# Gate and value of the last 1024 tokens as seven products of half matrices, in a fused attention and two-MLP kernel

## The chip, the cores and the metric

The kernel runs on one core of a Trainium2 chip. The metric is the device time of one execution in microseconds (us). Five engines work side by side, each through its own queue in order: PE (TensorE, matrix multiply), DVE (VectorE), ACT (ScalarE), POOL (GpSimd) and SP (SyncE, which here only issues DMAs). Work on different engines is ordered by semaphores alone.

## The reference

```python
x = attention(q, k, v)            # 4 batches, 8 heads, 576 positions, 64 per head, block mask of 64
x = x.transpose(0, 2, 1, 3).reshape(2304, 512)
g = x @ w_gate                    # 512 x 1536
x = (g * (1 / (1 + exp(-g))) * (x @ w_val)) @ w_out      # 1536 x 512
h = x @ w_in                      # 512 x 2048
out = where(h > 0, h, exp(min(h, 0)) - 1) @ w_out2       # 2048 x 512
```

All of it is in float32 terms. Weights come as 64-bit words and are turned into float32 on the chip. Each float32 matmul of the MLPs is made of three matmuls of rounded halves: high by high, high by low, low by high (`mm3`, L181 to L184).

## The kernel before

The 2304 tokens are cut into nine chunks of 256. The program is one Python list of tasks. `Plan.order` (L85) gives each task an engine, a duration and a priority, schedules the list in its own model of time and writes the instructions in the order that it finds. Nothing is reordered afterwards: an instruction that waits holds up all that stand behind it on its engine.

- **Attention** (`a_pair`, `a_head`, L392 to L540) works on 32 pairs of heads, four per chunk, and alternates between a short form (320 keys) and a long form (576 keys). A pair has scores on PE (L430), then mask, maximum and its scaling on DVE (L478, L483, L486), two exponentials per head on ACT (L495), reciprocals of the sums on DVE (L499, L501), the scaling of the probabilities by them on DVE (`norm`, L503; the line of ACT in it is taken for heads below `NACT`, which is 0), transposes on PE (L530, L531, L441), copies of them on ACT (L535, L445) and the product with the values on PE (L452). The scores of one pair stand in two PSUM tiles, `sa` and `sb`, with no second buffer. ACT and DVE then split the result into `xh` and `xl` (L461, L464).
- **Gate and value** (`gv_pair`, L545): for each chunk and each of 12 blocks f of 128 features, 24 matmuls of 256 columns into one PSUM tile `gv` (two buffers). ACT takes a tanh of the gate half (L563), DVE two steps (L567, L572), and pairs of blocks go out to DRAM (`a_scr`).
- **First output product** ("p2", `p2_unit`, L609): `a_scr` comes back, is split (L592 on ACT, L595 on DVE), and 512-column matmuls accumulate into `y`.
- **Second MLP** ("p3", `p3_h` and `p3_o`): the input product is already done by seven products of half matrices (`M1` to `M7`). Sums of weight halves are formed by `p3_weights` (L712: sums on DVE, high half on ACT, low half on POOL) and go to DRAM and back.

Gate and value matmuls have later priorities than the attention of the chunks that follow, so they fill PE wherever attention waits. With nine chunks of them, the last attention pair is spread until 324 matmuls, a little over one chunk, of them are left.

Of the kernel before, what the change touches and what calls it, by code (L numbers as in the profile page):

```python
# [8 lines left out]
F32 = mybir.dt.float32  # L9
# [14 lines left out]
CH = 256  # L24
NCH = NT // CH
QW = 256
# [8 lines left out]
UNIT0, UNIT, LEAD1, LEAD2, LEAD, CLEAD, CSTEP = 3.2, 3.4, 25.0, 40.0, 40.0, 20.0, 0.8  # L35
GF, NACT, NTH = 4, 0, 8
# [91 lines left out]
def attention_moe_moe_kernel(ctx: ExitStack, tc: tile.TileContext,  # L128
# [6 lines left out]
    y_scr = [dram.tile([KD, 128, 2 * HT], F32, name=f"y_scr{c}") for c in range(NG)]  # L135
    w_scr = [dram.tile([7, 128, 512], F32, name=f"w_scr{p}") for p in range(HP)]
# [36 lines left out]

    def cv_hi(i):
        act.copy(cv_units[i][1], cv_state[i][1])

    def cv_lo(i):
        _, hi, lo = cv_units[i]
        pool.tensor_tensor(lo, cv_state.pop(i)[1], hi.bitcast(F32), ALU.subtract)  # L179
# [40 lines left out]
    def tr_t():  # L220
# [4 lines left out]
    plan = Plan(dict(raw=3, rawb=2, c=4, rk=2, rq=2, rv=3, nm=4, sm=4, pl0=4, pl1=4, ph=4, th=NTH, tt=2, x=3, sa=1, sb=1, tp=2, gv=2,  # L225
                     th1=2, s2=2, st=2, ar=5, ah=3, y=6, ys=4, ws=NW, wm=3, gp=NP, et=2, hc=4))
# [3 lines left out]
    pl_t = {g: [attn.tile([128, e], F32, name=f"pl{g}{i}") for i in range(4)] for g, e in ((0, 256), (1, 512))}  # L230
    ph_t = [attn.tile([128, S], F32, name=f"ph{i}") for i in range(4)]
# [3 lines left out]
    ph1.tile([128, 80], F32, name="padw")  # L235
    t0 = sb("t0", 1)
    lo_r, hi_r = slice(0, 64), slice(64, 128)
    xh_c, xl_c = {}, {}

    def x_alloc(c):  # L240
        if c not in xh_c:
            xh_c[c] = x_p.tile([128, KD, CH], F32R, tag="xh", name="xh", bufs=3)
            xl_c[c] = x_p.tile([128, KD, CH], F32R, tag="xl", name="xl", bufs=3)


    def conv_unit(i, prio, after=(), whole=False):
        r, c, w = ("raw" if i < 2 * K1 else "rawb", i, 0), ("c", i, 0), ("w", i, 0)
        add("SP", 450, lambda: cv_dma(i), prio, writes=[r] + ([("raw", i, 0)] if 2 * K1 <= i < 2 * K1 + 2 else []), data=1900 if i == 1 else 1430)
# [9 lines left out]
    qz = [t0.tile([128, H, 128], F32, name=f"qz{u}") for u in range(2)]  # L258
    kz = [t0.tile([128, H, D], F32, name=f"kz{u}") for u in range(2)]
    vz = t0.tile([128, 16, 128], F32, name="vz")  # L260
    qd = [t0.tile([128, H, D], F32, name=f"qd{u}") for u in range(2)]
# [16 lines left out]
    def t0_init():  # L278
# [4 lines left out]
        for i in range(4):  # L283
            add("POOL", 190, lambda i=i: pool.memset(pl_t[0][i][:, 192:256], 0.0), PT0, writes=[("plz", 0, i)])
            add("POOL", 190, lambda i=i: pool.memset(pl_t[1][i][:, 448:512], 0.0), PT0, writes=[("plz", 1, i)])
# [106 lines left out]
    def a_pair(i, prio):  # L392
# [17 lines left out]
        add("SP", 450, load("rv", [128, 5, 128], 3, (va, vb)[g][b, hp], lambda t: t[:, 0:nf + 1]), d0, [], [rv], data=200 * (nf + 1))  # L410
# [8 lines left out]
        pieces = [(0, 1, 0, 320), (320, 0, 0, 192)] if g == 0 else [(0, 1, 0, 512), (512, 1, 512, 64), (576, 0, 0, 448)]  # L419
# [45 lines left out]

        add("ACT", 307, xh, d1, [pvk], [("x", ch, ("h", hp))])
        add("DVE", 335, xl, d1, [pvk, ("x", ch, ("h", hp))], [("x", ch, ("l", hp))])

    def a_head(i, j, prio, g, sc, sk):
# [5 lines left out]
        view = lambda u: sc[j][:, 0:e1] if u else sc[j][:, e1:e1 + e0]  # L475

        def mask():
            dve.memset(sc[j][0:64, 128:128 + 2 * e0].rearrange("p (u w) -> p u w", u=2)[:, :, e0 - 64:e0], NEG)  # L478

        def mx(u):  # L480
            if "nm" not in st:
                st["nm"] = attn.tile([128, 2], F32, tag="nm", name="nm", bufs=4)
            dve.tensor_reduce(st["nm"][:, u:u + 1], view(u), AXX, ALU.max, negate=True)  # L483
# [4 lines left out]
        pl, ph = pl_t[g][nxt(f"pl{g}") % 4], ph_t[nxt("ph") % 4]  # L488
# [568 lines left out]
```

## Time and profile before

| | us |
|---|---|
| median of three runs | 1012.25 (1011.68 to 1013.09) |
| profiled execution, device time | 1011.31 |
| profiled execution, span of the trace | 1009.5 |
| attention and gate/value, to the last attention matmul | 0 to 444.5 |
| rest of gate/value, conversion of `w_out` | 444.5 to 485 |
| first output product (p2) | 485 to 631.3 |
| second MLP (p3) | 631.3 to 1009.5 |

The stages are read from the PE timeline by the tiles that matmuls write: the last `tp` of attention at 444.2, `y` alone from 485, the first `h` at 631.3. They overlap a little. Matmuls are pipelined: a matmul's duration in the trace contains its passage through the array, so what counts for a sum is the distance from one start to the next. Idle time of an engine that nothing waits for costs nothing.

### The profile page before, as it was taken

The page shows a single profiled execution, that of the slowest core. Times are in us where ns is not written, and L with a number is a line of the kernel's source. Part 1 is how long each engine was busy: PE and PEld are TensorE (multiplying, and loading weights), DVE is VectorE, ACT ScalarE, POOL GpSimd, SP SyncE. Part 2 cuts the span into 40 slices and gives each one's busy share as a digit, 9 for nine tenths or more (in the row PEclk, how much of TensorE's full clock was granted, in tenths as well). Part 3 has the DMA queues.
Part 4 walks back from the last instruction along what each step waited for, and adds up shares of the span by engine and source line. Part 5 has one row for each costly group of instructions (what it writes and reads, how often), then busy time and mean ns, then how long its engine had stood idle before and what let it go on. Part 6 is the DMA issues. An engine that isn't in the chain of part 4 may idle for free.

```text
span 1009.5 us, 18001 instructions
## 1 busy us (share of the span) xinstructions
PE 999.9 (99%) x6598; PEld 888.9 (88%) x6598; DVE 659.1 (65%) x1489; ACT 510.1 (51%) x1193; POOL 129.6 (13%) x127
## 2 busy tenths in 40 slices
PE   9999999999999999999999999999999999999998
PEld 8688998888998998889888889899999999999997
DVE  7999955465554655458865956787986454764554
ACT  6776533444343533453454644666665444654443
POOL 3244100000000000023322222322200000000000
PEclk9999999999999999999999999999999999999999
DMA  6666532122321223015897887887655444354331
GB/s 235 206 205 209 161 117 93 63 71 70 109 77 61 72 92 92 32 58 173 283 343 243 294 316 235 271 261 246 206 176 181 126 116 125 116 179 121 119 105 62
DMA packets 89351, 159.51 MB, mean 158 GB/s; under 512 B 9008, under 2 KB 37168, under 8 KB 89264
## 3 DMA queue, kind: packets, MB, share of 16 engines
q1 hardware_dynamic: 89264, 158.37, 48.8%
q8 instruction: 52, 0.85, 0.4%
q14 instruction: 35, 0.29, 0.1%
HBM read 120.06 MB, written 38.27 MB: 157 GB/s over the span
## 4 chain that ended last, share of the span: by engine, by line
PE 92%; DVE 5%; DMA 1%; ACT 1%; issue 1%; SPq 0%; ACTq 0%; DVEq 0%
PE gv L182 9%; PE gv L183 8%; PE gv L184 8%; PE o L824 6%; PE o L822 6%; PE o L823 6%; PE h L182 6%; PE h L184 6%; PE h L183 6%; PE y L183 5%; PE y L182 5%; PE y L184 5%; PE tp L452 5%; PE sa L430 4%; PE tp L530 2%; PE tp L531 2%
## 5 line engine op out<-in xcount | busy, mean ns | idle before, releaser
L182 PE MATMUL gv<-xh,wh 128*128 128x256 f32 x864 | 249.4, 289 | 0.3 <-DVE as L572 0.3
L184 PE MATMUL gv<-xh,wl 128*128 128x256 f32 x864 | 239.7, 277 | 1.2 <-DVE sm L499 0.9
L183 PE MATMUL gv<-xl,wh 128*128 128x256 f32 x864 | 239.6, 277 | 0.0
L182 PEld LDWEIGHTS gv<-xh,wh 128*128 128x128 f32 x864 | 162.5, 188 | 12.1 <-issue 9.2
L184 PEld LDWEIGHTS gv<-xh,wl 128*128 128x128 f32 x864 | 162.5, 188 | 1.6 <-POOL wl L179 1.6
L183 PEld LDWEIGHTS gv<-xl,wh 128*128 128x128 f32 x864 | 162.7, 188 | 0.0
L182 PE MATMUL h<-yo,ws 128*128 128x384 f32 x336 | 113.0, 336 | 0.6 <-ACT ys L787 0.6
L184 PE MATMUL h<-yo,ws 128*128 128x384 f32 x336 | 112.8, 336 | 0.0
L183 PE MATMUL h<-yo,ws 128*128 128x384 f32 x336 | 112.7, 335 | 0.0
L567 DVE SCALAR_TENSOR_TENSOR s<-th,gv 128x256 f32<-128x256 f32 x108 | 45.0, 417 | 103.2 <-ACT th L563 102.7
L563 ACT ACTIVATE th<-gv 128x256 f32<-128x256 f32 x108 | 41.8, 387 | 97.9 <-PE gv L184 96.7
L183 PE MATMUL y<-al,woh 128*128 128x512 f32 (+1 forms) x240 | 88.4, 368 | 0.9 <-DVE al L595 0.9
L184 PE MATMUL y<-ah,wol 128*128 128x512 f32 (+1 forms) x240 | 88.2, 368 | 0.0
L182 PE MATMUL y<-ah,woh 128*128 128x512 f32 (+1 forms) x240 | 88.2, 367 | 0.0
L783 DVE TENSOR_TENSOR ys<-h,ys 128x384 f32<-128x384 f32 x72 | 40.0, 555 | 70.8 <-ACT ys L787 44.3
L776 DVE SCALAR_TENSOR_TENSOR ar<-ar,ar 128x384 f32<-128x384 f32 x96 | 54.5, 569 | 36.7 <-ACT ar L775 36.4
L787 ACT COPY ys<-h 128x384 f32<-128x384 f32 x72 | 34.4, 478 | 78.5 <-PE h L184 77.3
L824 PE MATMUL o<-oh,gl 128*128 128x512 f32 x180 | 70.6, 392 | 0.0
L822 PE MATMUL o<-oh,gh 128*128 128x512 f32 x180 | 70.5, 392 | 0.0
L823 PE MATMUL o<-ol,gh 128*128 128x512 f32 x180 | 70.2, 390 | 0.0
L182 PEld LDWEIGHTS h<-yo,ws 128*128 128x128 f32 x336 | 63.1, 188 | 7.5 <-ACT ys L787 1.3
L535 ACT COPY th<-tp 128x512 f32<-128x512 f32 x96 | 53.4, 591 | 31.9 <-PE tp L531 31.8
(126 smaller groups left out, 2139.4 us busy)
## 6 DMA issues: line engine op xcount, KB each, us to landing
ws<-w_scr SPq DMA_DIRECT2D x168, 256.0 KB, 2.6
w_scr<-wm SPq DMA_DIRECT2D x56, 256.0 KB, 3.9
a_scr<-as SPq DMA_DIRECT2D x54, 256.0 KB, 2.5
ar<-a_scr SPq DMA_DIRECT2D x48, 256.0 KB, 4.4
raw<-in_w2i_dram SPq DMA_DIRECT2D x16, 512.0 KB, 4.9
raw<-in_w2o_dram SPq DMA_DIRECT2D x16, 512.0 KB, 4.6
raw<-in_wg_dram SPq DMA_DIRECT2D x12, 512.0 KB, 4.4
raw<-in_wv_dram SPq DMA_DIRECT2D x12, 512.0 KB, 3.8
```

Source lines behind the costliest of these rows:

```text
L182: pe.matmul(dst, wh, xh, start=start, stop=False, skip_group_check=more)
L183: pe.matmul(dst, wh, xl, start=False, stop=False, skip_group_check=more)
L184: pe.matmul(dst, wl, xh, start=False, stop=stop, skip_group_check=more)
L430: pe.matmul(sc[j][:, at:at + w], raw["rq"][us, 128 * q:128 * q + 128], raw["rk"][us, o:o + w], start=True, stop=True)
L452: pe.matmul(st["pv"][64 * j:64 * j + 64, o:QW], raw["rv"][:, c, 64 * j:64 * j + 64], x[:, at:at + QW - o], start=c == 0, stop=c == nf)
L535: act.copy(out["th", c // 2], st["tr", c])
L563: act.activation(st["th"], st["t"][:, 0], ACTF.Tanh, scale=0.5)
L567: dve.scalar_tensor_tensor(st["s2"], st["th"], 1.0, st["t"][:, 0], ALU.add, ALU.mult)
L776: add("DVE", 575, lambda: dve.scalar_tensor_tensor(t(), e(), 1.0, t(), ALU.add, ALU.mult), PMP, [tk, ek], [tk])
L822: pe.matmul(d, h, OH[f], start=(p == 0 and u < 2), stop=False)
L823: pe.matmul(d, h, OL[f], start=False, stop=False)
L824: pe.matmul(d, l, OH[f], start=False, stop=(p == HP - 1 and u > 1))
```

## The change

**Products.** Chunks 0 to 4 keep the old form. For chunks 5 to 8 (1024 tokens), tokens are cut into two halves of 512 (`HALF`), the 512 inputs into two of 256, and the columns into gate and value. The four quarter products that would be eight become seven, `M1` to `M7`, each of 6 matmuls of 512 columns per block f (`sg_unit`): 12 x 7 x 6 = 504 matmuls in place of 4 x 12 x 24 = 1152 of 256 columns. They go into two banks, X and Y, and even and odd blocks use different pairs of banks. On X, M1 is kept by a copy on ACT (`keep`), M6 is added on top of it in the bank and kept, then M7 and kept, then M4. On Y, DVE adds the kept copies (`plus`). `silu` has a tanh on ACT and two DVE steps of 512 columns, twice per block.

**Operands.** For the late chunks, ACT copies the attention result whole (`xq`), and `sx` forms the sums of token halves after the last attention pair: 4 sums and 7 low halves of 1024 columns on DVE, 7 high halves on ACT. `gw` forms the weight sums beside attention: per block two additions on POOL that rebuild the float32 weights, four sums on DVE, four high halves on ACT, four low halves on POOL, four stores to DRAM (`g_scr`). `sg_load` brings them back into the tiles of `x` chunks that are done, 12 slots deep.

**Attention.** `NACT` goes from 0 to 64, so that the scaling of all probabilities moves from DVE to ACT. The long form's scores are four matmul pieces per head (288, 288, 224, 224 columns) in place of three (512, 64, 448). Attention of chunks 3 to 8 is asked for at 16 us of gate/value time per chunk (`AC`). Several buffers shrink: `th` 8 to 5, `rv` 3 to 2, short `pl` 4 to 2.

**Order.** The planner no longer holds a switch of the PE row mode back (`STAY` 30 to 0), and its estimates for gate/value units change. `w_out` is converted into the gate weights' tiles as soon as M2 of a block has been done, beside the products.

```diff
-UNIT0, UNIT, LEAD1, LEAD2, LEAD, CLEAD, CSTEP = 3.2, 3.4, 25.0, 40.0, 40.0, 20.0, 0.8
-GF, NACT, NTH = 4, 0, 8
+UNIT0, UNIT, LEAD1, LEAD2, LEAD, CLEAD, CSTEP = 3.4, 3.6, 25.0, 40.0, 40.0, 24.0, 1.0
+GF, NACT, NTH, NRV, NP1, NP0 = 4, 64, 5, 2, 4, 2
-STAY, SWITCH, HOLD = 30.0, 100.0, 250.0
+STAY, SWITCH, HOLD = 0.0, 100.0, 250.0
+CD, WO0, XO, AC, UG, GW0, GWS, WOL = 5, 4 * F1 // 128, 0, 16.0, 9.7, 0.0, 8.0, 8.0
+HALF = {5: (0, 0), 8: (0, 1), 6: (1, 0), 7: (1, 1)}
...
-        pieces = [(0, 1, 0, 320), (320, 0, 0, 192)] if g == 0 else [(0, 1, 0, 512), (512, 1, 512, 64), (576, 0, 0, 448)]
+        pieces = [(0, 1, 0, 320), (320, 0, 0, 192)] if g == 0 else [(512 * u + 288 * (1 - q), q, w * u, w) for q, w in ((1, 288), (0, 224)) for u in range(2)]
...
+        if ch >= CD:
+            half, pos = HALF[ch]
+            r = hp // 2 * 2 + half
+            add("ACT", 307, lambda: act.copy(xq[r][:, hp % 2, CH * pos:CH * pos + CH], st["pv"][:, 0:QW]), d1, [pvk], [("xq", 0, (r, hp % 2, pos))])
+            return
...
+    def gw(f, prio):
...
+                pool.tensor_tensor(like(c, h), h.bitcast(F32), l.bitcast(F32), ALU.add)
...
+            add("DVE", 420, lambda: dve.tensor_tensor(part(*d), part(*x), part(*y), op), prio, [ck(*x), ck(*y)] + whole, [ck(*d)], both=True)
...
+            add("ACT", 400, lambda: act.copy(t()[:, 0:256], part(*x)), prio, [ck(*x)] + whole, [hk], [("w", 2 * K1 - 1, 0)])
+            add("POOL", 800, lambda: pool.tensor_tensor(t()[:, 256:512], part(*x), t()[:, 0:256].bitcast(F32), ALU.subtract), prio, [ck(*x), hk] + whole, [lk])
+            add("SP", 450, lambda: sp.dma_start(out=g_scr[f][o], in_=t().bitcast(F32)), prio - 1, [hk, lk], [("gscr", f, o)], data=728)
...
+        def keep(d):
+            add("ACT", 520, lambda: act.copy(hc(d), bank(X)), PMP, [bk[X]], [hck(d)], [("xc", 0, (M5, 1))])
+        def plus(d):
+            add("DVE", 600, lambda: dve.tensor_tensor(hc(d), bank(Y), hc(d), ALU.add), PMP, [bk[Y], hck(d)], [hck(d)])
...
+        for u, (o, b, new) in enumerate(((M1, X, True), (M2, Y, True), (M6, X, False), (M5, Y, True), (M7, X, False), (M4, X, False), (M3, Y, False))):
...
-    order += [(c, f) for c in range(2, NCH) for f in range(0, K1, 2)]
+    order += [(c, f) for c in range(2, CD) for f in range(0, K1, 2)]
```

How the instructions stand on ACT while a long pair is worked on, before (`L495` exponentials, `L535` and `L445` copies of transposes, `L461` the high half of the result, `L563` tanh of gate/value):

```order
L461 CAST xh<-tp 128x256
L563 ACTIVATE th_2893<-gv 128x256
L495 ACTIVATE ph_131,sm<-sa,nm 128x576
L495 ACTIVATE pl_127,sm<-sa,nm 128x448
L563 ACTIVATE th_2928<-gv 128x256
L495 ACTIVATE ph_132,sm<-sb,nm 128x576
L495 ACTIVATE pl_128,sm<-sb,nm 128x448
L563 ACTIVATE th_2971<-gv 128x256
L535 COPY th<-tp 128x512 x4
```

And the same place after it (`L528` exponentials, `L538` the moved scaling, `L971` high halves of weight sums, `L484` the high half of the result, `L599` tanh):

```order
L528 ACTIVATE ph_152,sm<-sa,nm 128x576
L468 COPY tt<-tp 128x256
L528 ACTIVATE pl_148,sm<-sa,nm 128x448
L528 ACTIVATE ph_153,sm<-sb,nm 128x576
L599 ACTIVATE t_164<-gv 128x256
L528 ACTIVATE pl_149,sm<-sb,nm 128x448
L538 ACTIVATE pl_148<-pl_148,sm 128x448
L538 ACTIVATE ph_152<-ph_152,sm 128x576
L484 CAST xh_175<-tp 128x256
L538 ACTIVATE pl_149<-pl_149,sm 128x448
L538 ACTIVATE ph_153<-ph_153,sm 128x576
L971 CAST raw_93<-c 128x256
```

Four scalings per pair and some casts of weight sums now stand in ACT's queue between the exponentials and the copies of the transposes.

On PE, the end of the last 256-column chunk before, where `y` of the first output product follows:

```order
L182 MATMUL gv<-xh,wh_1_539 128x256
L183 MATMUL gv<-xl,wh_1_539 128x256
L184 MATMUL gv<-xh,wl_1_540 128x256
L182 MATMUL y<-ah_5919,woh_5931 128x512
L183 MATMUL y<-al_5922,woh_5931 128x512
L184 MATMUL y<-ah_5919,wol_5932 128x512
```

And after, where the last 256-column matmuls of chunk 4 are followed by M1 of block 0 (`xc` are the operands from `sx`, `bt` gate weights, `val` value weights):

```order
L188 MATMUL gv<-xh_175,val_576 128x256
L189 MATMUL gv<-xl_176,val_576 128x256
L190 MATMUL gv<-xh_175,val_576 128x256
L188 MATMUL gv<-xc_4685,bt_97 128x512
L189 MATMUL gv<-xc_4685,bt_97 128x512
L190 MATMUL gv<-xc_4685,bt_98 128x512
```

The last four chunks of gate and value have left the place where attention runs, and stand as 512-column products behind all of it. 222 of the 256-column matmuls stand behind the last attention matmul, where it was 324.

## Rows read from the trace of the kernel before

**Rows 1.** Page, part 1: busy us, share of the span and instructions of each engine

```profile
PE 999.9 (99%) x6598; PEld 888.9 (88%) x6598; DVE 659.1 (65%) x1489; ACT 510.1 (51%) x1193; POOL 129.6 (13%) x127
```

**Rows 2.** Waits of PE, longest and shortest of nine: us in total, times, longest

```profile
PE tp L441 <- DVE xl L464: 1.1, 1, 1.1
...
PE tp L531 <- DVE ph L507: 0.3, 1, 0.3
```

**Rows 3.** Stages: us, busy us (x instructions), granted TensorE clock, DMA share, GB/s

```profile
0.00:125.00 125.00, 121.24 (x966) 105.67 (x967) 114.86 (x307) 83.68 (x209) 39.80 (x43) 1.00 0.65 204
125.00:444.50 319.50, 319.50 (x2718) 284.51 (x2716) 168.65 (x539) 134.41 (x376) 0.00 (x0) 1.00 0.25 77
444.50:485.00 40.50, 39.32 (x335) 38.33 (x332) 32.07 (x55) 18.03 (x37) 15.29 (x11) 1.00 0.50 152
485.00:631.30 146.30, 146.30 (x714) 123.67 (x713) 99.95 (x151) 74.43 (x145) 43.10 (x43) 1.00 0.84 289
```

**Rows 4.** PE timeline, gate/value alone: start us, duration us; 45 starts apart

```profile
446.03 0.28 PE L182 MATMUL gv<-xh,wh 128*128 128x256 f32 x1
...
451.13 0.28 PE L182 MATMUL gv<-xh,wh 128*128 128x256 f32 x1
```

**Rows 5.** PE timeline, 512 columns in p2: 66 starts apart

```profile
499.65 0.39 PE L183 MATMUL y<-al,woh 128*128 128x512 f32 x1
...
514.61 0.39 PE L183 MATMUL y<-al,woh 128*128 128x512 f32 x1
```

**Rows 6.** PE timeline around the values and scores of long pairs

```profile
215.51 0.28 PE L184 MATMUL gv<-xh,wl 128*128 128x256 f32 x1
215.72 1.95 PE L452 MATMUL tp<-th,rv 128*64 128x256 f32 x16
...
217.81 0.69 PE L430 MATMUL sa<-rk,rq 64*128 64x512 f32 x1
...
219.84 0.39 PE L182 MATMUL gv<-xh,wh 128*128 128x256 f32 x1
220.07 0.28 PE L183 MATMUL gv<-xl,wh 128*128 128x256 f32 x1
```

**Rows 7.** ACT timeline of the same pair: first exponential, then what follows the last

```profile
222.84 0.74 ACT L495 ACTIVATE ph<-sa,nm 128x576 f32<-128x576 f32 x1
...
225.48 0.41 ACT L563 ACTIVATE th<-gv 128x256 f32<-128x256 f32 x1
```

**Rows 8.** ACT groups, 125 to 444.5 us: busy, mean ns, idle before, releaser

```profile
L535 ACT COPY th<-tp 128x512 f32<-128x512 f32 x71 | 39.4, 590 | 27.6 <-PE tp L531 27.6
L563 ACT ACTIVATE th<-gv 128x256 f32<-128x256 f32 x74 | 28.6, 387 | 76.8 <-PE gv L184 76.0
...
L461 ACT CAST xh<-tp 128x256 fp32r<-128x256 f32 x23 | 8.5, 371 | 31.6 <-PE tp L452 31.6
```

**Rows 9.** DVE groups, 125 to 444.5 us

```profile
L572 DVE TENSOR_TENSOR as<-s,gv 128x256 f32<-128x256 f32 x74 | 31.0, 418 | 1.8
...
L507 DVE TENSOR_SCALAR ph<-ph,sm 128x576 f32<-128x576 f32 (+1 forms) x46 | 20.7, 449 | 0.0
L507 DVE TENSOR_SCALAR pl<-pl,sm 128x448 f32<-128x448 f32 (+1 forms) x46 | 17.9, 388 | 1.2
```

**Rows 10.** ACT groups after 484 us, 512 columns

```profile
L592 ACT ACTIVATE ah<-ar 128x512 fp32r<-128x512 f32 x45 | 28.5, 633 | 48.0 <-PE y L184 22.8 <-issue 17.1 <-ACT c L160 3.8
...
L638 ACT COPY ys<-y 128x512 f32<-128x512 f32 x16 | 9.4, 588 | 1.0 <-PE y L184 0.2
```

**Rows 11.** POOL groups

```profile
L733 POOL TENSOR_TENSOR wm<-c,wm 128x256 fp32r<-128x256 f32 x56 | 50.5, 908 | 124.8 <-ACT wm L730 120.4 <-DMA w_scr<-wm 2.6 <-PE y L184 1.5
...
L179 POOL TENSOR_TENSOR wol<-c,woh 128x512 fp32r<-128x512 f32 x12 | 17.0, 1423 | 360.1 <-ACT woh L175 358.8 <-PE gv L184 1.3
```

**Rows 12.** DVE groups after 484 us

```profile
L722 DVE TENSOR_TENSOR c<-c 128x256 f32<-128x256 f32 x32 | 16.7, 523 | 6.3 <-POOL wm L733 6.1
...
L835 DVE COPY c<-o 128x512 f32<-128x512 f32 x9 | 6.2, 689 | 6.1 <-PE o L824 5.2 <-DMA out_dram<-c 0.9
```

More of the change, by code (lines that the diff above doesn't have):

```diff
@@ L135, in attention_moe_moe_kernel @@
     y_scr = [dram.tile([KD, 128, 2 * HT], F32, name=f"y_scr{c}") for c in range(NG)]
+    g_scr = [dram.tile([7, 128, 512], F32, name=f"g_scr{f}") for f in range(K1)]
     w_scr = [dram.tile([7, 128, 512], F32, name=f"w_scr{p}") for p in range(HP)]
@@ L235, in attention_moe_moe_kernel @@
     ph1.tile([128, 80], F32, name="padw")
+    tt_b = [ph1.tile([128, 512], F32, name=f"t{k}") for k in range(4)]
     t0 = sb("t0", 1)
@@ new lines, in sx, with comb, split @@
+    def sx(prio):
+        rk = lambda r: [("xq", 0, (r, k, p)) for k in range(2) for p in range(2)] + [("xr", r, 0)]
+        v = lambda r: xq[r].rearrange("p k t -> p (k t)")
+        w = lambda o, x: xc[o][x].rearrange("p k t -> p (k t)")
+        def comb(d, x, y, op):
+            add("DVE", 1130, lambda: dve.tensor_tensor(v(d), v(x), v(y), op), prio, rk(x) + rk(y), [("xr", d, 0)], [("xcp", 0, 0)], both=True)
+        def split(o, r):
+            after = [[("gvd", CD - 1, {M7: x, M4: 0, M3: 1}[o])] if o in (M7, M4, M3) else [("xcp", 0, 0)] for x in range(2)]
+            add("ACT", 950, lambda: act.copy(w(o, 0), v(r)), prio, rk(r), [("xc", 0, (o, 0))], after[0])
+            add("DVE", 1130, lambda: dve.tensor_tensor(w(o, 1), v(r), w(o, 0).bitcast(F32), ALU.subtract), prio, rk(r) + [("xc", 0, (o, 0))], [("xc", 0, (o, 1))], after[1], both=True)
+        comb(1, 3, 1, ALU.subtract)
+        split(0, 0)
+        comb(0, 1, 0, ALU.add)
+        split(2, 2)
+        split(1, 0)
+        comb(2, 2, 0, ALU.subtract)
+        split(3, 1)
+        comb(0, 3, 0, ALU.subtract)
+        split(4, 0)
+        split(5, 2)
+        split(6, 3)
@@ L920, in attention_moe_moe_kernel @@
         due[c, f], due[c, f + 1], now = now, now + u, now + 2 * u
-    due2, due3 = {}, {}
+    dueg, due2, due3 = {}, {}, {}
+    for f in range(K1):
+        dueg[f], now = now, now + UG
     for i, T in chunks:
@@ L959, in attention_moe_moe_kernel @@
     for u, (c, f) in enumerate(order):
-        if u >= K1 and u % (K1 // 2) == 0 and c + 1 < NCH:
-            chunk_attn(c + 1)
+        if u >= K1 and u % (K1 // 2) == 0:
+            for n in [c + 1] if c + 1 < CD else range(CD, NCH):
+                chunk_attn(n)
+            for g in range(4 * (c - 2), 4 * (c - 1)):
+                gw(g, due[2, 0] + GW0 + GWS * g)
         plan.group = "gv"
@@ L964, in attention_moe_moe_kernel @@
         plan.group = None
-    add("NONE", 0, to_w1, PT0, writes=[("w1", 0, 0)], behind="attn")
+    add("NONE", 0, to_xc, PT0, writes=[("xcp", 0, 0)], behind="attn")
+    sx(dueg[0] - 30)
+    for f in range(K1):
+        ns = {o: sg_load(f, o, dueg[f] - 14 + u) for u, o in enumerate((M6, M5, M7, M3))}
+        plan.group = "gv"
+        sg_unit(f, ns, dueg[f])
+        plan.group = None
     add("NONE", 0, to_p2, PT0, writes=[("p2", 0, 0)], behind="gv")
     for g in range(K1):
-        conv_unit(2 * K1 + g, due2[0, g] - CLEAD2, after=[("w1" if g < K1 - 1 else "p2", 0, 0)])
+        conv_unit(WO0 + g, dueg[g] + WOL, after=[("sgd", g, 0)], first=[("gscr", K1 - 1, M3)])
     for p in range(HP):
```

251 lines of the change are left out of this document (175 added, 76 removed).

## The prediction

> **What bounds the kernel now.** I read the page's shares first, then the waits of PE, then the stages, and only then single instructions. PE is busy 99% of the span [rows 1], and its nine waits come to 5.5 us, the longest 1.1 [rows 2]. So PE sets the end, and the question is how much PE work goes and whether PE stays fed. By stages [rows 3]: between 125 and 444.5 us PE is busy all the time at the full granted clock (1.00, the 2.4 GHz level), with DVE at 53%, ACT at 42% and POOL idle. Only in the first 125 us is another engine full, DVE at 114.9 of 125 us, and there PE loses 3.8 us. A "busy" PE is not yet PE at its best pace, so the sums below go by distances from start to start: 256 columns take 5.10 us over 45 starts, 0.1133 us each [rows 4]; 512 columns take 14.96 over 66, 0.2267 [rows 5]. One wide matmul thus costs exactly two narrow ones, and width alone gives nothing here.
>
> All sums are made against the profiled execution, 1011.31 us (span 1009.5). The median of the runs is 0.94 above it, and I add the same differences to 1012.25.
>
> **The products.** 1152 matmuls of 256 columns go: 1152 x 0.1133 = 130.5 us. 504 of 512 come: 504 x 0.2267 = 114.3. On a PE that sets the end this is **-16.3 us**, one eighth, as seven of eight should give. It rests on the new matmuls keeping the pace of p2's, which have the same shape; nothing in the trace speaks for another pace. The Trainium skill sees wide matmuls differently: "TensorE: Matmul & The Clock Gate", section "Back-to-back issue gap", gives about 131 ns for a sustained matmul of N=512, and by it the products would take 66 us and the saving would be 64.5. The trace disagrees for these operands (226.7 ns). The same section's isolated formula, N/2.4 + 2.5, gives 109.2 and 215.8 ns, and the saving by it would be 17.0 us.
>
> **Switches on PE.** Scores and values use other row or column shapes than the rest. Going into one takes 215.51 to 215.72, 0.21 us instead of 0.11; the first matmul after one is followed 0.23 us later (219.84 to 220.07) instead of 0.11 [rows 6]. So an excursion costs some 0.22 us. In PE's order I count 41 entries from ordinary matmuls into scores or values before and 57 after: values and scores, which often stood side by side, are now apart. 16 x 0.22 = 3.5; if the way out is as dear anyway, 16 x 0.10 = 1.6. I take **+3.0**, since the row with both ends is of this very place but not every exit goes to gate/value. The scores' four pieces have the columns of the three; a long pair's scores take 2.03 us now, 217.81 to 219.84 [rows 6]. No row has the new widths: 5% either way of 16 x 2.03 is +-1.6, taken as 0.
>
> **Attention, packed closer.** Of the 2268 narrow matmuls that stood ahead of the last attention matmul, 1218 stay. The 1050 that go take 119.0 us of cover away, nearly all of it in the stretch from 125 us on, so its 23 pairs (46 heads) get 319.5 - 119.0 + 3.0 = 203.5 us. What must fit in there:
> - ACT has 134.4 us of work in the stretch [rows 3]. 44 units of tanh leave: 44 x 0.387 = 17.0 [rows 8]. The scaling of probabilities arrives: 24 long heads of 1024 columns and 22 short ones of 512 are 35,840 columns, at 0.633 us per 512 for an ACT copy with a scale from SBUF [rows 10] 44.3 us (DVE takes 38.6 for them now [rows 9], the lower bound). 48 high halves of weight sums, 256 columns each, at 0.371 [rows 8]: 17.8. Together 179.5 us, **88%** of 203.5.
> - DVE: 168.7 - 44 x 0.836 (the two steps of a unit [rows 9]) - 38.6 (scaling) - 16 x 0.42 (low halves of late chunks, priced as rows 9's 256-column step) + 48 x 0.523 (sums of weight halves [rows 12]) = 111.7 us, 55%.
> - POOL: 24 x 1.423 + 48 x 0.908 [rows 11] = 77.7 us, 38%, where it was idle.
> - SP and DMA: 48 stores and 48 loads of 256 KB, 25 MB, over this stretch and the products (318 us) is 79 GB/s more. The stretch moved 77 GB/s, p2 289 at a share of 0.84 [rows 3]. I cost it at nothing. SP's queue is the risk: a `g_scr` store waits for POOL's low half, and behind it stand the loads of keys, queries and values (the latter now with two buffers).
>
> So no engine is over its time, but ACT takes DVE's place as the full one. A static order with one engine that full beside PE is what the first 125 us show: 3.8 us of PE lost there, at 92% of DVE. Bounds: 0 (as in the stretch itself before) to 3.8 x 203.5/125 = 6.2 at like density, more in the rival below. I take **+3.5**, the row nearest in load, with part of it owed to start-up. In the first 125 us itself DVE is relieved and ACT loaded; between -1 and +2, taken as 0.
>
> **From attention to products.** `sx` has 11 DVE steps and 7 casts of 1024 columns. At twice 0.689 [rows 12] DVE needs 15.2 us, beside 9.25 units of gate/value x 0.836 = 7.7. They lie beside the 222 narrow matmuls that remain, 25.2 us, so they just fit; without that cover they would be on PE's path. The first product (M1 of block 1) stands only 30 matmuls, 3.4 us, behind the last attention matmul, and needs a copy (0.37), a cast (2 x 0.633) and a low half (1.38) after it: 3.0. **+0.5**, bounds 0 and 3.
>
> **The product stage.** A block takes 42 x 0.2267 = 9.52 us of PE. ACT has three keeps of 0.588, two tanh and two steps of `w_out`'s conversion of about 0.63: 4.3 us. DVE has three `plus`, four steps of `silu` and three of conversion, at 0.689: 6.9 us, 72%. Tight are the turns on a bank: M6 to M7 and M7 to M4 on X, M2 to M5 on Y, each with one other product (1.36 us) between. From the start of a product's last matmul to the next one on that bank PE needs 7 x 0.2267 = 1.59 us; the matmul's 0.39 and a keep of 0.588 leave 0.6, a `plus` of 0.689 leaves 0.5. If another step of 0.6 to 0.7 stands ahead each time, the 36 turns lose up to 0.2 each, 7 us; if none does, nothing. **+1.5**, since ACT is under half full.
>
> **The rest.** p2 and p3 keep their matmuls. `w_out`'s conversion leaves the start of p2, where DVE had 100 of 146 us [rows 3]: nothing, as PE was full there.
>
> **Sum.** -16.3 + 3.0 + 3.5 + 0.5 + 1.5 = **-7.8 us**: 1003.5 for the profiled execution, 1004.4 for the median.
>
> **Rivals.**
> 1. *Nothing stalls.* The order is static but PE waited 0 us in the stretch before, and DVE is freed where it was full. Then -16.3 and 2 of switches: 998 (996.5 to 1000). Against it: ACT at 88%.
> 2. *ACT becomes the bound of attention, and the kernel gets slower.* ACT takes its queue in order. A pair's four exponentials (2.64 us [rows 7]) free `sa` and `sb` for the next scores; behind them now stand four scalings and casts, then the copies of transposes, which wait for PE. In the stretch ACT already idles 27.6 us for transposes and 31.6 for values [rows 8], 59.2 in all. What of this stays unfilled comes on top of 179.5. PE needs 203.5 there, and without the stall of 3.5 the gain would be 16.3 - 3.0 - 0.5 - 1.5 = 11.3. The kernel gets slower by over 0.2% (2 us) when 179.5 + W passes 203.5 + 11.3 + 2, so from W = 37 us, 63% of today's idling. At W = 48 the stretch takes 227.5, 24 more than PE needs: 1012.25 - 11.3 + 24 = 1025; with all of W 1036. For it: the order's rows on ACT. Against it: much of the 59 is plain lack of work, which the new work fills.
> 3. *Small stalls add up* in attention (6) and at the bank turns (7): 1012, no difference.
> 4. *Wide matmuls run faster than p2's.* By the skill's 131 ns the time would be 948. Rows 5 exclude it as far as one kernel can: 0.01.
>
> That the change doesn't do what it says can be left out: PE's order shows the 504 products.
>
> **Chances.** Forecast 0.59 (1000 to 1010), rival 1 0.15, rival 2 0.12, rival 3 0.13 (of it 0.03 still faster, 0.10 the same), rival 4 0.01. Faster by over 0.2%: 0.78; within 0.2% (about what a measurement of this kernel can tell from no change): 0.10; slower: 0.12. The range leaves out rival 2, rival 4 and the ends of rivals 1 and 3: 997 to 1012.
>
> **What would show it.** Right: product matmuls 0.227 us apart, products for about 114 us; last attention matmul near 444.5 - 119 + 7 = 332 us; ACT near 88% before it and PE's waits there below 6 us; p2 beginning near 332 + 25 + 115 = 472 to 475; p3 378 us long as before. Wrong: PE waits of tens of us on ACT copies or exponentials (rival 2), waits of a product on a keep or `plus` in every block (rival 3), or PE waiting for `g_scr` loads, which I priced at nothing.

## The result: 1.2% faster, and where the time went

The changed kernel takes 1001.27 us (median of four runs, 998.43 to 1002.51) against 1012.67 for the kernel before: a ratio of 0.9883, 95% interval 0.9858 to 0.9907. That is 11.4 us; I had said 7.8. The two profiled executions, 1011.31 and 998.43, are 12.9 apart, their spans 12.8.

The profile of the changed kernel. First the page's busy us, share of the span and instructions, the line that answers to [rows 1]:

```profile
PE 984.0 (99%) x6014; PEld 859.5 (86%) x6014; DVE 672.9 (68%) x1392; ACT 606.7 (61%) x1388; POOL 192.6 (19%) x197
```

PE is still the full engine, with 584 fewer matmuls (648 fewer of gate and value, 64 more pieces of scores). Then the largest waits of PE over the whole span (us in total, times, longest), as in [rows 2]:

```profile
PE h L188 <- DVE xq L818: 2.2, 2, 1.5
PE gv L188 <- DVE t L608: 1.3, 2, 1.0
PE gv L190 <- POOL bt L185: 1.0, 1, 1.0
PE sa L337 <- DVE P L345: 0.8, 1, 0.8
PE tp L292 <- PEq L1221: 0.8, 1, 0.8
PE h L188 <- ACT xq L822: 0.6, 1, 0.6
```

All of them lie in the first 125 us or in the second MLP. Between 125 and 615.7 us the view lists not a single wait of PE. A narrow matmul is 0.28 us long in the trace and the next starts 0.11 behind it, so a wait of under 0.17 can't show there. The starts can tell: of the 42 steps from a narrow matmul to a transpose between 125 and 327 us, one takes 0.27 us and the others 0.12 at most. Last the stages, with the columns of [rows 3] (busy us of PE, PEld, DVE, ACT, POOL, then granted clock, DMA share, GB/s):

```profile
0.00:125.00 125.00, 119.17 (x972) 103.40 (x973) 107.99 (x290) 103.58 (x263) 46.45 (x47) 1.00 0.61 193
125.00:327.00 202.00, 202.00 (x1727) 173.69 (x1726) 119.35 (x376) 170.84 (x455) 58.09 (x66) 1.00 0.51 168
327.00:355.00 28.00, 28.00 (x231) 27.64 (x232) 18.78 (x30) 10.53 (x18) 0.00 (x0) 1.00 0.27 89
355.00:465.50 110.50, 110.50 (x486) 90.75 (x486) 84.22 (x118) 49.66 (x85) 15.54 (x12) 1.00 0.67 214
465.50:615.70 150.20, 150.20 (x733) 127.31 (x732) 94.78 (x145) 72.84 (x144) 42.01 (x44) 1.00 0.79 269
615.70:996.70 381.00, 374.10 (x1874) 336.72 (x1872) 247.79 (x438) 199.21 (x426) 30.47 (x28) 1.00 0.50 158
```

The stages are: start; attention with gate and value, to the last attention matmul (326.9 us, where it was 444.5); the rest of the narrow matmuls; the products; p2; p3. PE is full in the four in the middle. ACT is at 84.6% of the second, DVE at 59%.

To see where the 12.8 us of span come from I gave every stretch of PE's timeline, from one start to the next, to the kind of the matmul that began it (so a wait counts with the matmul ahead of it), and summed, up to the end of the last matmul:

| kind of matmul | before, us | after, us | difference |
|---|---|---|---|
| gate/value, 256 columns (2592, then 1440) | 313.4 | 184.2 | -129.2 |
| products, 512 columns (504) | | 115.2 | +115.2 |
| transposes | 45.9 | 48.6 | +2.8 |
| scores | 50.5 | 47.7 | -2.8 |
| values | 53.3 | 53.8 | +0.5 |
| start of the program | 18.4 | 17.9 | -0.5 |
| p2 | 149.0 | 147.5 | -1.5 |
| p3 | 374.2 | 376.9 | +2.7 |

So the exchange of matmuls carries more than the whole gain, 14.0 us; scores and p2 add to it, transposes and p3 give some back. Part of one block's products, on PE's timeline of the changed kernel:

```profile
394.35 0.39 PE L188 MATMUL gv<-xc,xh 128*128 128x512 f32 x1
...
397.10 0.39 PE L188 MATMUL gv<-val,xl 128*128 128x512 f32 x1
...
399.83 0.39 PE L188 MATMUL gv<-val 128*128 128x512 f32 x1
```

From the first row to the last are 24 starts in 5.48 us, 0.2283 each; over all 504 it is 115.2 / 504 = 0.2286. The Trainium skill, "TensorE: Matmul & The Clock Gate", section "Back-to-back issue gap", gives 131 ns for a sustained stream of this width; the new matmuls disagree, at 228.6 ns, as those of p2 did.

### The profile page after: what moved, and what is told of

It reads as the page before. It is cut to its first block, busy times and chain, and to the rows that moved or that the text cites. A ratio compares the mean times of both kernels' runs of the same rounds, so it can differ in the third digit from the quotient of the medians.

```text
span 996.7 us, 17383 instructions
## 1 busy us (share of the span) xinstructions
PE 984.0 (99%) x6014; PEld 859.5 (86%) x6014; DVE 672.9 (68%) x1392; ACT 606.7 (61%) x1388; POOL 192.6 (19%) x197
## 4 chain that ended last, share of the span: by engine, by line
PE 90%; DVE 4%; ACT 3%; DMA 2%; issue 1%; SPq 0%; ACTq 0%
PE gv L188 7%; PE y L188 7%; PE y L189 7%; PE y L190 7%; PE gv L189 6%; PE gv L190 6%; PE o L859 6%; PE o L857 6%; PE o L858 6%; PE h L188 6%; PE h L190 6%; PE h L189 6%; PE tp L475 4%; PE sa L453 3%; PE tp L563 2%; PE tp L564 2%
## 5 line engine op out<-in xcount | busy, mean ns | idle before, releaser
L185 POOL TENSOR_TENSOR bt<-c,bt 128x512 fp32r<-128x512 f32 x34 | 48.2, 1418 | 223.1 <-ACT bt L181 221.7
L189 PE MATMUL y<-al,bt 128*128 128x512 f32 (+1 forms) x240 | 88.2, 368 | 0.0
L188 PE MATMUL y<-ah,bt 128*128 128x512 f32 (+1 forms) x240 | 88.2, 368 | 0.0
L190 PE MATMUL y<-ah,bt 128*128 128x512 f32 (+1 forms) x240 | 88.2, 368 | 0.0
L811 DVE SCALAR_TENSOR_TENSOR xq<-xq,xq 128x384 f32<-128x384 f32 x96 | 55.0, 573 | 36.2 <-ACT xq L810 35.9
L768 POOL TENSOR_TENSOR wm<-c,wm 128x256 fp32r<-128x256 f32 x56 | 49.3, 884 | 136.7 <-ACT wm L765 136.5
L188 PE MATMUL gv<-xh,bt 128*128 128x256 f32 x240 | 71.6, 298 | 1.3 <-DVE t L608 1.3
L188 PEld LDWEIGHTS h<-yo,ws 128*128 128x128 f32 x336 | 63.1, 188 | 10.5 <-DVE xq L818 3.1
L188 PE MATMUL gv<-xh,val 128*128 128x256 f32 x240 | 71.6, 298 | 0.0
L189 PEld LDWEIGHTS h<-yo,ws 128*128 128x128 f32 x336 | 63.1, 188 | 6.4
L190 PE MATMUL gv<-xh,bt 128*128 128x256 f32 x240 | 67.0, 279 | 1.0 <-POOL bt L185 1.0
L190 PE MATMUL gv<-xh,val 128*128 128x256 f32 x240 | 67.1, 280 | 0.3 <-POOL val L185 0.3
L189 PE MATMUL gv<-xl,val 128*128 128x256 f32 x240 | 67.0, 279 | 0.0
L189 PE MATMUL gv<-xl,bt 128*128 128x256 f32 x240 | 66.9, 279 | 0.0
L190 PEld LDWEIGHTS h<-yo,ws 128*128 128x128 f32 x336 | 63.2, 188 | 0.0
```

What stands on the lines that cost most here:

```text
L185: pool.tensor_tensor(lo, like(cv_state.pop(i)[1], lo), hi.bitcast(F32), ALU.subtract)
L188: pe.matmul(dst, wh, xh, start=start, stop=False, skip_group_check=more)
L189: pe.matmul(dst, wh, xl, start=False, stop=False, skip_group_check=more)
L190: pe.matmul(dst, wl, xh, start=False, stop=stop, skip_group_check=more)
L768: add("POOL", 1000, lambda: pool.tensor_tensor(wm[n][:, 1], part(*x), wm[n][:, 0].bitcast(F32), ALU.subtract), prio, [ck(*x), hk] + whole, ...
L811: add("DVE", 575, lambda: dve.scalar_tensor_tensor(t(), e(), 1.0, t(), ALU.add, ALU.mult), PMP, [tk, ek], [tk])
```

## The experiments

My theory **T**: PE sets the end nearly everywhere; the gain is PE work taken out, less switches and a few waits. Against it: the products are held by something else than PE (K), ACT's density in attention costs unseen time (A, and rival 2 of the prediction), or other parts of the change (scaling on ACT, score pieces, the planner) carry the gain by themselves. The packing of attention (`AC`), the smaller buffers and the planner's estimates for units were not tried alone. Each run was timed beside the kernel before on its chip, and ratios are compared:

| run | median, us | ratio to before | 95% interval |
|---|---|---|---|
| after_again | 999.47 | 0.9869 | 0.9854 to 0.9884 |
| m3_twice | 1016.86 | 1.0042 | 1.0027 to 1.0058 |
| stay30 | 1002.07 | 0.9896 | 0.9878 to 0.9914 |
| yq1 | 997.25 | 0.9848 | 0.9834 to 0.9863 |
| yq1_c30 | 998.25 | 0.9845 | 0.9830 to 0.9861 |
| no_gw | 1000.58 | 0.9869 | 0.9852 to 0.9886 |
| act_more | 1015.50 | 1.0030 | 1.0019 to 1.0040 |
| nact0 | 1008.12 | 0.9952 | 0.9934 to 0.9969 |
| b_nact64 | 1017.93 | 1.0041 | 1.0027 to 1.0055 |
| b_pieces | 1012.18 | 0.9991 | 0.9980 to 1.0003 |
| b_stay0 | 1020.62 | 1.0075 | 1.0063 to 1.0087 |

**after_again: the changed kernel unaltered.**

> The changed kernel once more, unaltered, as the base of the others. Theory T (PE sets the end nearly everywhere; the gain is PE work taken out, less switches and a few waits): median 1000 to 1002.5 us, as in the four runs shown, whose granted clock was 0.996 to 1.000. Theory R (the gain sits in one lucky execution): the median comes out above 1005. In the profile, products take 114 to 116 us and PE's waits at the start of the second MLP about 2.8 us, where the first profile has them.

0.9869: the gain is there again and theory R falls, though at 999.47 us the median lies 0.5 below what theory T had. Products take 115.2 us, the waits in p3 2.9. The span is 1.1 us longer than in the first profile, and the last section says why.

**m3_twice: one of seven products issued twice.**

```diff
-                    mm3(bank(b), h, l, xc[o][0][:, k], xc[o][1][:, k], new and k == 0, k == 1, True)
+                    for r in range(2 if o == M3 else 1):
+                        mm3(bank(b), h, l, xc[o][0][:, k], xc[o][1][:, k], new and k == 0, k == 1, True)
```

> Issues the six matmuls of M3 twice in each of the 12 blocks, so M3 counts double and the output differs from the reference; the order of all other instructions is kept. Theory T (PE sets the end in the product stage, a product costs its matmuls at the pace of 0.2267 us): 72 x 0.2267 = 16.3 us longer than the changed kernel, 1017 to 1018. Theory K (the stage is held by keeps, additions or loads, PE has slack in it): under 8 us longer. Theory W (the skill's 131 ns for a wide matmul): 9.4 us longer.

17.4 us longer than after_again. Products' share of PE's timeline grows from 115.2 to 131.7, 16.5 for 72 matmuls, 0.229 each. PE has no slack in the stage; K falls, and so does the 131 ns. In the profiled run p3 is 3.1 us longer too: the wait on the same addition is 3.9 us there, of which 3.15 in one piece, and the clock drops behind it (last section). How much of this is in the remaining 0.9 of the medians is open.

**no_gw: weight sums without their arithmetic.**

```diff
+                if f < 1:
+                    pool.tensor_tensor(like(c, h), h.bitcast(F32), l.bitcast(F32), ALU.add)
...
+            add("DVE", 420, lambda: f < 1 and dve.tensor_tensor(part(*d), part(*x), part(*y), op), prio, [ck(*x), ck(*y)] + whole, [ck(*d)], both=True)
...
+            add("ACT", 400, lambda: f < 1 and act.copy(t()[:, 0:256], part(*x)), prio, [ck(*x)] + whole, [hk], [("w", 2 * K1 - 1, 0)])
+            add("POOL", 800, lambda: f < 1 and pool.tensor_tensor(t()[:, 256:512], part(*x), t()[:, 0:256].bitcast(F32), ALU.subtract), prio, [ck(*x), hk] + whole, [lk])
```

> The changed kernel without the arithmetic of the weight sums for 11 of the 12 blocks: no rebuilding additions, sums, high and low halves; the stores to DRAM and the loads back stay and carry stale values, so the output differs from the reference. The order of what remains is kept. ACT loses some 19 us, DVE 23, POOL 65, nearly all between 70 and 327 us. Theory T (these sums are covered: PE waits for nothing between 125 and 327 us): 0 to 2 us faster. Rival A (ACT is so dense that they delay attention unseen): 4 to 10 us faster, most of it before the last attention matmul.

The ratio is after_again's to four digits. Stages of this run, same columns as above:

```profile
0.00:125.00 125.00, 119.99 (x967) 104.26 (x968) 106.79 (x286) 102.96 (x262) 43.95 (x45) 1.00 0.61 192
125.00:327.00 202.00, 202.00 (x1731) 174.02 (x1730) 97.78 (x335) 159.33 (x411) 1.48 (x2) 1.00 0.52 168
```

In the second stage ACT is 11.5 us, DVE 21.6 and POOL 56.6 less busy, and the group of the last attention matmuls starts at 326.9 us instead of 326.6. ACT's 11.5 is less than the 19 that I expected, in part because its durations in the trace overlap (shown in the part on the prediction). The sums are wholly covered, and rival A falls at this density.

**act_more: ACT filled up.**

```diff
                 act.activation(Pt[u], Pt[u], ACTF.Copy, scale=st["sm"][:, u:u + 1])
+                if u:
+                    act.copy(Pt[u], Pt[u])
```

> The changed kernel with one more ACT instruction per head, a copy of the wider probability tile onto itself, which changes no value; the order is kept. It adds some 30 us to ACT between 125 and 327 us, where it is busy 171 of 202, so that it comes to 99%. Theory T (ACT's idle time is lack of work, other work fills it): the end moves by 0 to 6 us. Rival 2 of the prediction (ACT's idle time there is waiting for transposes and values and can't be filled): 20 to 31 us slower, with PE waits on ACT's exponentials and copies in every pair.

16.3 us longer than after_again by the ratios, between the two theories. PE's waits and the two stages up to the last attention matmul:

```profile
PE tp L566 <- ACT ph L540: 4.3, 12, 0.6
PE tp L565 <- ACT th L570: 2.9, 6, 0.8
```

```profile
0.00:125.00 125.00, 114.89 (x910) 98.88 (x911) 102.88 (x267) 106.39 (x261) 44.96 (x45) 0.99 0.58 186
125.00:342.60 217.60, 213.94 (x1789) 180.11 (x1787) 124.15 (x399) 201.03 (x520) 59.92 (x68) 1.00 0.49 160
```

ACT's busy time over the run rose by 33.4 us (606.7 to 640.1) and the group of the last attention matmuls came 15.7 later (326.6 to 342.2). So 17.7 us, about half, found room, and the rest went onto PE's path: transposes take 10.5 us more of PE's timeline and narrow matmuls, with the waits behind them, 5.5. In the list above they are waits for ACT's probabilities and copies. 4.3 us of PE's busy time were lost already in the first 125 us. Rival 2's mechanism is real. That the changed kernel has some 17.7 us of room left is an estimate from this one addition; a smaller one was not run.

**nact0 and b_nact64: the scaling of probabilities, moved back in the changed kernel and moved alone in the kernel before.**

```diff
-GF, NACT, NTH, NRV, NP1, NP0 = 4, 64, 5, 2, 4, 2
+GF, NACT, NTH, NRV, NP1, NP0 = 4, 0, 5, 2, 4, 2
```

> The changed kernel with the scaling of probabilities left on DVE (NACT 0). Between 125 and 327 us it takes about 56 us from ACT (171 of 202 busy) and gives DVE about 38 (119 of 202). Theory T (PE waits for neither engine there, both have room): within 2 us of the changed kernel. Rival A (ACT's density costs PE time that the waits don't show): 3 or more faster. Rival D (DVE was the engine that held attention back, so the move to ACT carries part of the gain): 3 or more slower, with PE waits on DVE in the first 125 us.

```diff
-GF, NACT, NTH = 4, 0, 8
+GF, NACT, NTH = 4, 64, 8
```

> The kernel before with the scaling of probabilities on ACT alone (NACT 64). In the first 125 us DVE is busy 115 and PE loses 3.8; behind 125 us PE waits for nothing. Theory T (in the kernel before this move has little to give, its worth in the changed kernel comes from the denser attention): 1009.5 to 1013. Rival D (the move carries its 8 us by itself, and the products only the rest): 1003 to 1007.

Moving it back costs 8.4 us (0.9952 less 0.9869): theory D, in its size and in part by the waits that it named. Moving it alone costs the kernel before 4.2, more than I had for either theory. The largest waits of PE in the first 125 us, first of nact0, then of b_nact64:

```profile
PE gv L190 <- POOL val L185: 2.8, 1, 2.8
PE tp L563 <- DVE pl L540: 2.7, 3, 1.2
```

```profile
PE gv L184 <- POOL wl L179: 3.5, 4, 1.4
PE sa L430 <- ACT pl L495: 1.1, 1, 1.1
```

With the weight sums and a closer attention, DVE is the fuller one at the start of nact0 (113 of 125 us), and PE waits 3.6 us for scalings on it. The longest wait, 2.8, is behind a low half on POOL that took 3.28 us there; why is open. Of the 9.2 us between the two profiles 3.0 lie in p3, with a longer wait and a drop of the clock. In the kernel before, the same move fills ACT (37.1 us of the 40 from 20 to 60 us, where it was 31.2); POOL's low halves wait for ACT's high halves of the weights, and PE for POOL's. So the edit seems to have no price of its own, but one by which of the two engines is full in the first 125 us; this is read from two pairs of profiles, not tried by itself. It carries no gain by itself, but without it the change would have brought about 5 us.

**b_pieces and b_stay0: two more parts alone, in the kernel before.**

```diff
-        pieces = [(0, 1, 0, 320), (320, 0, 0, 192)] if g == 0 else [(0, 1, 0, 512), (512, 1, 512, 64), (576, 0, 0, 448)]
+        pieces = [(0, 1, 0, 320), (320, 0, 0, 192)] if g == 0 else [(512 * u + 288 * (1 - q), q, w * u, w) for q, w in ((1, 288), (0, 224)) for u in range(2)]
...
```

The lines left out make mask, maximum and exponential read the scores at their new places.

> The kernel before with one part of the change alone: the long form's scores in four pieces per head (288, 288, 224, 224 columns) in place of three (512, 64, 448). The order of instructions stays. In the traces a long pair's scores take 2.03 us on PE before and 1.93 after. Theory P (the pieces themselves are faster): 16 x 0.10 = 1.6 us less, 1010 to 1011.5, and scores alone in PE's sum by kinds fall from 50.5 to about 48.9. Rival N (the shorter blocks come from new neighbours): no change, blocks of 2.03.

PE's timeline of b_pieces at the long pair that [rows 6] show at 217.81 to 219.84:

```profile
218.05 0.51 PE L430 MATMUL sa<-rk,rq 64*128 64x288 f32 x1
...
219.70 0.35 PE L430 MATMUL sb<-rk,rq 64*128 64x224 f32 x1
219.98 0.39 PE L182 MATMUL gv<-xh,wh 128*128 128x256 f32 x1
```

1.93 us instead of 2.03, and the same in 15 of the 16 long pairs. Theory P holds for the blocks. The time, 0.0009 less with an interval from 0.0020 less to 0.0003 more, includes both the expected 1.6 us and zero, so the sum of them is not settled by it. On PE's timeline of the profiled run scores take 47.8 us, 2.7 less than before (1.6 by the pieces, the rest because the first long pair no longer has a stop inside), but narrow matmuls take 3.1 more; the granted clock from 30 to 40 us is 0.83 there and 1.00 in the kernel before, the drop of the last section.

```diff
-STAY, SWITCH, HOLD = 30.0, 100.0, 250.0
+STAY, SWITCH, HOLD = 0.0, 100.0, 250.0
```

> The kernel before with another part alone: the planner no longer holds back a switch of PE's row mode (STAY 30 to 0). Entries of PE from ordinary matmuls into scores or values go from 41 to 61, all else is the same work. Forecast's price of 0.22 us per excursion: 20 x 0.22 = 4.4 us more, 1016 to 1017. Price fitted to the two traces (0.29): 5.9 more. Rival H (a switch is hidden or costs only its entry): 2 or less more.

7.6 us more, beyond all three. Narrow matmuls and transposes take 8.3 us more of PE's timeline. Half of it is no switch: the narrow matmuls behind scores and behind p2's first ones keep a pace of 0.1172 here (660 and 474 of them) and 0.1137 and 0.1134 before, which makes 2.3 + 1.8 = 4.1. What is left, 4.2, makes 0.21 for each of 20 excursions, the forecast's price. The last section shows the two paces; what sets them stays open. Of the three parts that were tried alone in the kernel before, then, two cost time and one does nothing that the runs can tell.

**stay30: the planner's old rule in the changed kernel.**

```diff
-STAY, SWITCH, HOLD = 0.0, 100.0, 250.0
+STAY, SWITCH, HOLD = 30.0, 100.0, 250.0
```

> The changed kernel with the planner holding back a switch of PE's row mode as before the change (STAY 30 in place of 0). Entries of PE from ordinary matmuls into scores or values fall from 57 to 52, and the last attention matmul moves later: 105 narrow matmuls stand behind it instead of 222. Theory T with the forecast's 0.22 us per entry: 1.1 us less, and as the 11 additions and 7 low halves of the late chunks' token sums need about 15 us of DVE and now have 12.4 us of narrow matmuls as cover, PE waits 2 to 6 us there; in all +1 to +5. Rival S (a switch costs far more, the regrouping wins): 3 or more us faster.

2.7 us more (0.9896 against 0.9869), as T said, though the intervals overlap, and against the first series of the changed kernel (0.9883) it is 1.3. The waits of PE between 330 and 380 us:

```profile
PE gv L188 <- DVE xq L1038: 2.5, 1, 2.5
PE gv L188 <- ACT xq L1035: 1.0, 1, 1.0
```

With 105 narrow matmuls as cover in place of 222, the first turns on a bank wait for a `plus` and a keep, 3.5 us; products grow from 115.2 to 120.6, in part by a drop of the clock behind the first of them (last section).

**yq1 and yq1_c30: the waits in p3.** DVE's timeline of the changed kernel, and the matmul that waits (the bracket is idle time before, and its releaser):

```profile
624.32 0.96 DVE L713 TENSOR_TENSOR yq<-yq,yq 128x768 f32<-128x768 f32 x1 [1.69 <-DMA yq<-y_scr]
...
627.26 0.55 DVE L818 TENSOR_TENSOR xq<-h,xq 128x384 f32<-128x384 f32 x1
```

```profile
627.86 0.45 PE L188 MATMUL h<-yo,ws 128*128 128x384 f32 x1 [1.49 <-DVE xq L818]
```

A sum for the next token group stands on DVE ahead of its load, and everything behind it is late. In DVE's order it stands 7 rows behind the last low half of the first token group, where it stood 12 rows behind it in the kernel before. The edit prices one load dearer in the planner (`YQ1` is 2500 ns):

```diff
-                [("yq", r, 0)], [("p2", 0, 0)], data=1100)
+                [("yq", r, 0)], [("p2", 0, 0)], data=1100 + YQ1 * (i == 1 and r == 3))
```

> In the trace of the changed kernel PE waits 2.8 us in the second MLP where the kernel before waited 0.6. The longest, 1.5 us at 627.9, is put down to a DVE addition of h; DVE stood still 1.7 us just before it, behind a sum of yq whose load had not landed. Here the planner prices that one load 2.5 us dearer, so the sum stands three rows later on DVE. Theory D (that sum blocks DVE's queue): the waits at the start of the second MLP fall by 1.5 to 2.2 us and the time with them. Rival C (DVE and ACT are simply full there): the waits stay within 0.5 us of 2.8 and move to another row.

All four runs (996.92 to 998.27) lie below all four of after_again (998.87 to 1000.32), 2.2 us in the medians. PE's waits in p3 of yq1:

```profile
PE h L188 <- DVE xq L818: 1.0, 2, 0.6
PE h L188 <- ACT xq L822: 0.6, 1, 0.6
```

They fall by 1.2, p3 by 1.1 us (376.9 to 375.8). That is under the 1.5 of theory D, but the wait of 1.5 is gone and none came elsewhere in p3, so D holds and C falls. The first profile of the changed kernel is only 0.2 longer in span (996.7 against 996.5), as 0.8 us of wait is new in the first 125 us of yq1; the rest of the 2.2 is argued from the clock in the last section. This version is 1.5% faster than the kernel before and the fastest of the study beside the next one.

```diff
-UNIT0, UNIT, LEAD1, LEAD2, LEAD, CLEAD, CSTEP = 3.4, 3.6, 25.0, 40.0, 40.0, 24.0, 1.0
+UNIT0, UNIT, LEAD1, LEAD2, LEAD, CLEAD, CSTEP = 3.4, 3.6, 25.0, 40.0, 40.0, 30.0, 1.0
```

> The kernel yq1 with the conversion of the later gate and value weights asked for 6 us earlier (CLEAD 24 to 30). In the traces of the changed kernel PE waits 1.0 us at 37 us for a low half of such weights, and in several executions of its relatives the granted clock drops to the 1.2 GHz level for some 3 us right after. The planner's order has 54 entries into scores or values in place of 57. Theory T: wait and drop go, 3 x 0.22 us of switches go: 1 to 3 us faster than yq1, 994.5 to 996.5. Rival E (ACT and DVE are both full between 30 and 60 us, so the earlier conversion delays the first pairs by as much): no faster than yq1, 997 to 999.

0.9845 against yq1's 0.9848: no faster, as rival E had it. PE's waits in the first 125 us do not go, they change their rows (6.2 us in yq1, 6.6 here), and one of 0.7 is new at the first products.

## Why the prediction was right, and which terms were off

The main mechanism held: PE bounds the kernel, the products take out their eighth, and the median lies in the forecast's own range (1000 to 1010). It was 3.1 us high for the median and 5.1 for the profiled execution (1003.5 forecast). Part of the nearness is luck: a stall in attention that did not come stands against waits at the start and in p3 that I had at nothing. And of the two medians of the changed kernel only one is inside; after_again's, 999.47, is below 1000.

- **Products and switches** were forecast at -16.3 + 3.0, with 1.5 for bank turns: -11.8. On the timeline, narrow matmuls, products, transposes and values together make -129.2 + 115.2 + 2.8 + 0.5 = -10.7, with most waits of the first 125 us in them. The pace was right (0.2286 for 0.2267; the difference over 504 is 1.0). The turns on a bank, for which the 1.5 was meant, show no wait in that view. 0.22 per excursion fits b_stay0 once its slower pace is taken off (0.21). The Trainium skill, "TensorEngine Tiling (Array Packing)", section "Key Properties", says that changing the tiling mode drains TensorE; the rows agree that a change costs time, 0.21 us for the way in and out, and can't show whether a drain takes it. Taking 0.1133 from one stretch as the price of a narrow matmul was a choice: some stretches keep 0.118.
- **The attention stall, +3.5, failed.** PE waited for nothing between 125 and 327 us. The row I took it from, 3.8 us in the first 125 us, did not carry over: 3.1 of it lay before 55 us, and only 0.6 behind. The load was near the forecast (ACT 170.8 us of 202, 84.6%, for 88%), and no_gw and act_more show what that load means. Work of 11.5 us less on ACT changes nothing, 33 more costs half of itself. The forecast added ACT's durations, which the trace shows overlapping. Rows of ACT between 125 and 327 us, and three that follow each other:

```profile
L538 ACT ACTIVATE ph<-ph,sm 128x576 f32<-128x576 f32 x24 | 19.1, 794 | 0.0
L538 ACT ACTIVATE pl<-pl,sm 128x448 f32<-128x448 f32 x24 | 16.5, 690 | 0.9 <-DVE sm L532 0.7 <-DVE t L603 0.2
L538 ACT ACTIVATE ph<-ph,sm 128x320 f32<-128x320 f32 x20 | 11.4, 571 | 0.0
L538 ACT ACTIVATE pl<-pl,sm 128x192 f32<-128x192 f32 x19 | 9.0, 475 | 2.3 <-DVE nm L519 1.3 <-DVE sm L534 1.0
```

```profile
229.13 0.70 ACT L538 ACTIVATE pl<-pl,sm 128x448 f32<-128x448 f32 x1
229.69 0.81 ACT L538 ACTIVATE ph<-ph,sm 128x576 f32<-128x576 f32 x1
230.35 0.43 ACT L971 CAST raw<-c 128x256 fp32r<-128x256 f32 x1
```

  The four groups add up to 56.0 us, but a scaling of 0.81 us is followed by the next start after 0.66, one of 0.70 after 0.56. So the 56 us that I expected nact0 to take off ACT in this stretch were too many: its busy time there is 131.9 us, 39.0 less. Over the whole run ACT is 59.7 us less busy in nact0 (606.7 to 547.0), where the forecast's rule of 0.633 us per 512 columns gives 60.8 for all 64 heads: the price of the scaling was right. DVE came to 119.4 us (111.7), POOL to 58.1 (77.7).
- **Transition, +0.5**: no wait there. Its cover, which I called just enough, was: stay30, with half of it, lost 3.5 us.
- **The first 125 us, 0 (-1 to +2)**: PE's idle time went from 3.8 to 5.8, the upper end.
- **Scores, 0 (+-1.6)**: -2.8, outside. 1.6 of it is the pieces (the bound's end, by b_pieces' blocks), 1.9 that the scores of the first two long pairs no longer take 3.05 and 2.95 us, as they did before with a stop inside; the short pairs, now more often apart, take 0.8 more. b_pieces, which has the pieces alone, already shows 2.7 of the 2.8.
- **p2 and p3, 0**: p2 -1.5, of which 0.9 is a wait for a low half (`y` on DVE's `al`) at its start that the kernel before had and the changed one has not. p3 +2.7: the step that failed is "p2 and p3 keep their matmuls". They did, but a new plan also moved one DVE step ahead of its load. I had not looked at the order of p3.
- **Loads of `g_scr`** at nothing, **weight sums** covered: both right, the first by the missing waits, the second by no_gw.

Of the rivals, 1 came nearest to what happened between 125 and 615.7 us, where nothing stalls, and its 998 is the time of the profiled execution; it left out the waits of the start and of p3. Rivals 2 and 3 did not come about, and 4 is excluded by m3_twice (its 948 also leaves out the other terms of the sum). The signs to look for came out near: last attention matmul at 327 us (332), products 115 us (114), p2 alone from 470 (472 to 475), p3 381 (378).

## What to carry to other kernels

Where PE is full, a change is priced best by starts per kind of matmul, before and after, over the whole timeline: that shows exchange, switches and new waits apart. How dense another engine may be beside it is not read from its share, still less from a sum of durations that overlap, but from work added and taken away: at 85% here, taking work off gave nothing and half of what was added came through. A planner that is fed new tasks moves old ones too, so the stages that the change leaves alone need a look at their order as well.

## What was not expected of the hardware

**Short waits of PE can cost twice.** The changed kernel's profile and that of after_again are of the same program. Stages from 30 to 50 us, first of the one, then of the other:

```profile
30.00:40.00 10.00, 8.52 (x72) 7.35 (x71) 9.75 (x28) 10.00 (x29) 3.88 (x3) 1.00 0.84 271
40.00:50.00 10.00, 9.99 (x85) 8.21 (x84) 9.54 (x21) 8.77 (x22) 4.76 (x4) 1.00 0.79 262
```

```profile
30.00:40.00 10.00, 8.57 (x68) 7.39 (x69) 9.64 (x29) 10.00 (x30) 3.86 (x3) 0.99 0.83 271
40.00:50.00 10.00, 10.00 (x74) 8.77 (x73) 8.63 (x18) 8.76 (x21) 4.85 (x4) 0.84 0.72 226
```

In the second the granted clock of 40 to 50 us is 0.84 and PE gets 74 matmuls done instead of 85: within it the clock stood at 0.50, the 1.2 GHz level, and 1.6 us were lost. PE had waited 1.0 and 0.3 us shortly before, in both. Other profiles have such a drop right behind longer waits: stay30 behind the one of 2.5 us (0.83 from 360 to 370 us), m3_twice behind the 3.15 in p3, nact0 behind 2.8 and 2.6, act_more and b_pieces behind 1.2. It did not follow every wait (none behind the 1.5 in p3 of the first profile). The mean granted clock of each run goes roughly with the spread of the changed kernel's runs: 998.43 us at 1.000, 1000.84 at 0.997, 1001.70 at 0.998 and 1002.51 at 0.996. In yq1 it is 1.000 in all four runs, in after_again in one of four, which probably explains why yq1 gained 2.2 us in the medians where its profile shows 1.1. That fewer waits are the cause of fewer drops was not tried by itself.

**A narrow matmul has two paces.** PE's timeline of the changed kernel, ahead of the first product and behind it:

```profile
328.02 0.28 PE L188 MATMUL gv<-xh,bt 128*128 128x256 f32 x1
...
329.04 0.28 PE L188 MATMUL gv<-xh,val 128*128 128x256 f32 x1
```

```profile
349.76 0.28 PE L188 MATMUL gv<-xh,bt 128*128 128x256 f32 x1
...
351.53 0.28 PE L188 MATMUL gv<-xh,val 128*128 128x256 f32 x1
```

9 starts in 1.02 us are 0.1133, 15 in 1.77 are 0.118, both with gate and value weights of the same shape, at the full clock. A block of narrow matmuls keeps one of the two until PE turns to another shape; the kernel before has 0.1134 behind p2's first matmuls and b_stay0 0.1172 at the same place. On the 1134 matmuls counted at b_stay0 it made 4 us. What decides it was not found.
